# Loading k transposed by DMA in a long-convolution and token-MLP kernel

## The chip, the cores and the metric

One core of a Trainium2 chip runs the program. The metric is the time of one execution on the device, in microseconds (us); the kernel before takes 172.17 us (median of three runs, 172.11 to 172.44). The core has five engines that run side by side, each through its own list of instructions in order: TensorE (PE, matrix products; loading the stationary operand is shown as PEld), VectorE (DVE), ScalarE (ACT), GpSimd (POOL) and SyncE (SP, which here only issues DMA transfers). Products land in PSUM, which has eight banks; only DVE and ACT empty it into SBUF, the working memory of 128 partitions.

## The reference

What is computed, with S = 2048 tokens, D = 448 channels, F = 1792, all inputs bf16:

```python
x  = A_q                                   # [1, S, D]
# A: a four-tap filter along the tokens of k, a product with v, a long convolution, a gate
k_shift = sum(k_pad[:, t:t + S, :] * shift_k[:, 3 - t] for t in range(4))
kv = k_shift * v
y  = irfft(rfft(kv, 2 * S) * rfft(ssm_k, 2 * S))[:S] + kv * ssm_D     # per channel, along the tokens
h  = x + layernorm(x) * y
# B: an MLP over the tokens
n  = layernorm(layernorm(h))
u  = gelu(einsum("bsd,sf->bdf", n, w1) + b1)
h2 = h + transpose(einsum("bdf,fs->bds", u, w2) + b2)
```

## The kernel before

Token s = 16 q + r sits on partition q (0 to 127), in row r (0 to 15); so a tensor of 2048 x 448 is [128, 16, 448] in SBUF, and a load of four rows (a chunk, g = 0 to 3) moves 448 KB. The convolution is done as a two-step Fourier transform by table products on TensorE, with transfers inside SBUF between the steps (the shuffles, L1075 and L1202).

The steps carry tags, which the written order uses:

- `tables`: GpSimd and DVE make phase numbers (L838, L842, L845), ACT makes sines of them (L848, two halves of the table E, and L863).
- `kT`: the state kernel ssm_k (KN, [channel, token], four blocks of 128, 128, 128 and 64 channels) is turned by TensorE (L1038), eight rows to a PSUM bank, and emptied by `evac` (ACT L739, DVE L742) into KT.
- `kv`: the filter. L966 turns k (KH) into KX, channel on the partition: 48 transposes of 128 channels and 32 of 64; eight evictions (`kv.1` to `kv.8`) follow. L951 makes the 64 x 64 diagonals DG of the filter's taps, and L992 multiplies shifted stretches of KX by them, so that the filtered k comes out with the token on the partition; DVE multiplies it with v straight from PSUM (L1007), two instructions for each of eight chunks (four g, two halves cc of the channels). A zero column at the left of rows 13 to 15 stands for the tokens before the first.
- `k1`, `u1` (L1059): the first product of the transform, of the state kernel and of kv. Sixteen steps each, four products of 32 columns side by side; L1069 (ACT or DVE) empties two banks, and for the first four of `k1` L1067 (DVE) adds ssm_D. Every second step sends its shuffle (L1075), two transfers from GpSimd's queue and one from SyncE's.
- `k2`, `u2` (L1094): the second product, emptied by L739, L740, L742 and L743.
- `q`, `xn`: statistics of x (L1238, L1240) and its normalized rows (L1271 on ACT).
- `i1` (L1161, L1178), the shuffle back (L1202, L1189) and `i2` (L1304, L1310): the product of both transforms and the way back, with the gate and the second layernorm behind it.
- `mlp`: L1436 and L1446 (first matrix, GELU at L1426), L1458 (second matrix) and L1461, the final sum.

Which instruction comes when is written out by hand: the dictionary ORDER names, for each engine, every operation by step and number, and SLOTS gives each step its PSUM banks (two numbers a step, the second a bank or the first of a pair) and its ring buffers. The program computes only the waits. An engine never overtakes: an operation that waits holds up all that stand behind it in its list. `dummy` products (L1025) keep TensorE at work while nothing else is there.

SyncE's list begins with two chunks of k (0 and 1), the four blocks of the state kernel, ssm_D and the biases, the other chunks of k, v2, the filter, v3, v1 and v0. TensorE's list begins with nine dummies, the turning of the first k chunks, then the state kernel:

```python
"dummy.0:1-9 kv.4:0-11 kv.3:0-7 kv.6:0-11 kv.5:0-7 kT.1:0-7 kT.0:0-3 kT.1:9-11 kT.0:4-7 kT.3:0-7 "
...
"k1.9:0-7 k1.12:0-7 k1.10:0-7 kv.1:0-7 kv.2:0-11 k1.11:0-7 k1.15:0-7 k1.14:0-7 k1.13:0-7 kT.4:0-7 "
"kv.8:0-11 kv.12:0-23 kv.9:0-27 kv.10:0-23 kv.11:0-27 k1.4:0-7 k1.0:0-1 u1.0:0-7 k1.0:2-7 u1.1:0-7 "
```

Of the kernel before, what the change touches and what calls it, by code (L numbers as in the profile page):

```python
# [36 lines left out]
    ),  # L37
    "act": (
# [9 lines left out]
    ),  # L48
    "dve": (
# [15 lines left out]
    ),  # L65
    "pool": (
# [512 lines left out]
def _build(nc, A_q, A_k, A_v, A_shift_k, A_ssm_k, A_ssm_D, B_w1, B_b1, B_w2, B_b2, out):  # L579
# [8 lines left out]
    R = 16  # L588
# [39 lines left out]
    o_BD = o_IH + 256  # L628
    o_SM = o_BD + 4 * 256
    SMALL = o_SM  # L630
    NSMALL = 4032

    ctx = ExitStack()
    with ctx:
# [886 lines left out]
```

## Time and profile before

| | |
|---|---|
| median of three runs | 172.17 us |
| the profiled execution | 171.71 us |
| its span, first to last instruction | 169.7 us |
| PE busy | 159.8 us (94%) |
| DVE busy | 104.1 us (61%) |
| ACT busy | 88.4 us (52%) |
| POOL busy | 60.4 us (36%) |
| granted TensorE clock | 1.00 |
| read from HBM | 22.05 MB |

The profile is of one execution. A group of instructions shows the source line, engine, operation, output and inputs with shapes, how often, the busy time, the mean of one in ns, and the idle time of the engine just ahead of it with what ended it. SBUF is one tensor here, named arena, and PSUM one, named ps. Busy shares are means over stages with different limits; what counts for an edit is the stage in which it lies. Rows on one engine may overlap, since the next instruction starts while the last one still drains.

### The profile page before, as it was taken

The page shows a single profiled execution, that of the slowest core. Times are in us where ns is not written, and L with a number is a line of the kernel's source. Part 1 is how long each engine was busy: PE and PEld are TensorE (multiplying, and loading weights), DVE is VectorE, ACT ScalarE, POOL GpSimd, SP SyncE. Part 2 cuts the span into 40 slices and gives each one's busy share as a digit, 9 for nine tenths or more (in the row PEclk, how much of TensorE's full clock was granted, in tenths as well). Part 3 has the DMA queues.
Part 4 walks back from the last instruction along what each step waited for, and adds up shares of the span by engine and source line. Part 5 has one row for each costly group of instructions (what it writes and reads, how often), then busy time and mean ns, then how long its engine had stood idle before and what let it go on. Part 6 is the DMA issues. An engine that isn't in the chain of part 4 may idle for free.

```text
span 169.7 us, 3575 instructions
## 1 busy us (share of the span) xinstructions
PE 159.8 (94%) x1419; PEld 93.5 (55%) x1419; DVE 104.1 (61%) x193; ACT 88.4 (52%) x128; POOL 60.4 (36%) x155
## 2 busy tenths in 40 slices
PE   6999999788998899979999999999999999999994
PEld 2786745324333343434455555555567777777783
DVE  7998998999999999999987730000003223132231
ACT  3597859789999999998976144102360000000000
POOL 8346717473780554695788540000000000000000
PEclk9999999999999999999999999999999999999999
DMA  5999899775648875666999999940000111101111
GB/s 161 421 351 366 264 287 346 272 271 211 208 121 280 288 210 152 191 187 210 393 394 400 420 423 422 415 180 0 0 0 4 54 54 54 54 0 58 54 54 54
DMA packets 15564, 35.15 MB, mean 207 GB/s; under 512 B 3804, under 2 KB 9644, under 8 KB 15548
## 3 DMA queue, kind: packets, MB, share of 16 engines
q1 hardware_dynamic: 12396, 28.26, 45.6%
q0 software_dynamic: 3008, 6.58, 12.2%
q8 instruction: 11, 0.18, 0.4%
q10 hardware_dynamic: 144, 0.08, 0.2%
q14 instruction: 5, 0.04, 0.1%
HBM read 22.05 MB, written 1.84 MB: 141 GB/s over the span
## 4 chain that ended last, share of the span: by engine, by line
PE 68%; ACT 13%; DMA 8%; POOL 4%; DVE 3%; issue 2%; DVEq 0%; ACTq 0%; POOLq 0%
PE ps L1458 25%; PE ps L1436 13%; PE ps L1446 12%; ACT arena L739 8%; DMA arena<-arena 8%; PE ps L1025 3%; POOL arena L1075 3%; ACT arena L1069 3%; PE ps L966 3%; PE ps L1310 3%; PE ps L1059 3%; PE ps L1038 3%; ACT arena L740 2%; PE ps L992 2%; PE ps L1178 2%
## 5 line engine op out<-in xcount | busy, mean ns | idle before, releaser
L1461 DVE SCALAR_TENSOR_TENSOR arena<-ps,arena 128x448 bf16<-128x448 f32 (+2 forms) x17 | 11.1, 656 | 55.9 <-PE ps L1458 55.9
L1458 PE MATMUL ps<-arena 128*128 128x448 bf16 (+2 forms) x238 | 42.7, 342 | 0.0
L1458 PEld LDWEIGHTS ps<-arena 128*128 128x128 bf16 x238 | 33.3, 145 | 9.5
L1436 PE MATMUL ps<-arena 128*128 128x448 bf16 x112 | 23.7, 353 | 0.1
L739 ACT CAST arena<-ps 128x896 bf16<-128x896 f32 (+1 forms) x29 | 23.3, 896 | 0.6 <-PE ps L1178 0.4
L1069 ACT CAST arena<-ps 128x896 bf16<-128x896 f32 x24 | 20.4, 913 | 5.4 <-PE ps L1059 5.1
L1446 PE MATMUL ps<-arena 128*128 128x448 bf16 x112 | 22.5, 352 | 0.0
L1075 POOL DMA_DIRECT2D arena<-arena x32 | 17.6, 555 | 13.7 <-ACT arena L1069 13.5
L1426 ACT ACTIVATE arena<-ps,arena 128x448 bf16<-128x448 f32 x14 | 7.9, 641 | 18.2 <-PE ps L1436 10.6
L1059 PE MATMUL ps<-arena 128*32 128x448 bf16 x256 | 14.8, 355 | 2.3 <-ACT arena L1069 0.9
L1161 DVE TENSOR_TENSOR arena<-arena 128x1792 bf16<-128x1792 bf16 x16 | 16.6, 1082 | 0.2
L1436 PEld LDWEIGHTS ps<-arena 128*128 128x128 bf16 x112 | 10.8, 98 | 10.6 <-DVE arena L1389 0.7
L1446 PEld LDWEIGHTS ps<-arena 128*128 128x128 bf16 x112 | 11.0, 98 | 10.2
L1094 PE MATMUL ps<-arena 128*64 128x448 bf16 x128 | 15.1, 359 | 0.9 <-ACT arena L739 0.4
L1178 PE MATMUL ps<-arena 64*128 64x448 bf16 x128 | 14.1, 351 | 1.4 <-ACT arena L739 0.7
L1202 POOL DMA_DIRECT2D arena<-arena x16 | 9.3, 588 | 12.7 <-ACT arena L739 12.7
L1094 PEld LDWEIGHTS ps<-arena 128*64 128x64 f16 x128 | 5.6, 108 | 9.8 <-ACT arena L739 2.8
L1358 ACT ACTIVATE arena<-arena 128x448 bf16<-128x448 f32 x14 | 8.0, 572 | 5.6 <-DVE arena L1330 5.4
L1059 PEld LDWEIGHTS ps<-arena 128*32 128x32 f16 x256 | 5.3, 95 | 9.7 <-ACT arena L1069 2.5
L1178 PEld LDWEIGHTS ps<-arena 64*128 64x128 f16 x128 | 5.3, 94 | 9.7 <-DVE arena L1161 3.6
L1238 DVE BATCH_NORM_STATS2 arena<-arena 128x6 f32<-128x448 bf16 x16 | 9.6, 610 | 0.0
L1389 DVE TENSOR_SCALAR arena<-arena 128x448 bf16<-128x448 f32 x16 | 7.8, 507 | 2.7 <-POOL arena L1382 2.7
(98 smaller groups left out, 192.5 us busy)
## 6 DMA issues: line engine op xcount, KB each, us to landing
arena<-in_B_w_dram SPq DMA_DIRECT2D x8, 896.0 KB, 10.0
arena<-in_B_w_dram SPq DMA_DIRECT2D x2, 2048.0 KB, 17.3
arena<-arena SPq DMA_DIRECT2D x16, 224.0 KB, 3.5
arena<-arena POOLq DMA_DIRECT2D x32, 112.0 KB, 3.5
arena<-in_B_w_dram SPq DMA_DIRECT2D x2, 1536.0 KB, 19.2
arena<-arena POOLq DMA_DIRECT2D x13, 196.0 KB, 4.6
arena<-in_A_k_dram SPq DMA_DIRECT2D x4, 448.0 KB, 5.3
arena<-in_A_v_dram SPq DMA_DIRECT2D x4, 448.0 KB, 8.5
```

The costliest lines, as they stand in the source:

```text
L739: return e.copy(out=dst(), in_=src())
L1059: op("pe", lambda e, W, b=b, r=r, q=q, x=x, c0=c0: e.matmul(PS[32 * q:32 * q + 32, b.slots[x], 0:D], E[:, 2 * r + x, c0:c0 + 32], src[:, r ...
L1069: return e.copy(out=dst, in_=Ppair(b)) if W == "act" else e.tensor_copy(out=dst, in_=Ppair(b))
L1075: shuf[tag].append(op(q_, lambda e, W, g=g, i=i, a=a, nu=nu, jh=jh: e.dma_start(T[a + i:a + i + 4 * nu - 3:4].rearrange("p (j k) c d -> p ...
L1094: op("pe", lambda e, W, b=bs[h], h=h, j=j, c=c, par=par: e.matmul(PS[64 * par:64 * par + 64, b.slots[c], 0:D], FW[:, 64 * c:64 * c + 64], ...
L1161: op("dve", lambda e, W, m=m, i=i: e.tensor_tensor(out=MR(m.slots[0]).rearrange("p (x y) d -> p x y d", x=2), in0=TU[:, i].unsqueeze(2).br ...
L1178: k = op("pe", lambda e, W, b=bs[h], m=ms[h], par=par, t=t, tab=tab, xy=xy, P=P: e.matmul(Pb(b, par), tab[P, :], MR(m.slots[0])[P, xy, :], ...
L1238: op("dve", lambda e, W, bs=bs, r=r: e.bn_stats(out=bs, in_=XR(r)), r=[(oX(r), DB)], w=[(ob, 24)], n=D, kind="1x")
L1436: op("pe", lambda e, W, r=r, fc=fc, b=bs[fc]: e.matmul(Pb(b), W1A[:, r, 128 * fc:128 * fc + 128], Q[:, r, :], start=(r == 0), stop=(r == R ...
L1446: op("pe", lambda e, W, r=r, fc=fc, b=b: e.matmul(Pb(b), W1B[:, r, 128 * (fc - n0):128 * (fc - n0) + 128], Q[:, r, :], start=(r == 0), sto ...
L1458: op("pe", lambda e, W, r=r, fc=fc, b=b, d0=d0, d1=d1: e.matmul(Pb(b)[:, d0:d1], W2[fc // 7][:, fc % 7, r:S:R], G[:, fc, d0:d1], start=(fc ...
L1461: op("dve", lambda e, W, r=r, b=b, A=A, d0=d0, d1=d1: e.scalar_tensor_tensor(out=XR(r)[:, d0:d1], in0=Pb(b)[:, d0:d1], scalar=bm[:, r:r + ...
```

## The change

k is no longer loaded with the token on the partition. Four DMA transfers on SyncE's queue, behind the state kernel and the filter, write it transposed into KX, at the place of KH: a chunk of four rows is [128 tokens, 4 x 448 columns], cut into 14 groups of 128 columns; each group's 128 columns land on the partitions and its 128 tokens side by side. So the 80 transposes on TensorE and their eight evictions go away. As 448 is 7 x 64, a block of 64 channels lies on the lower or the upper half of the partitions by the parity of 7 (r mod 4) + block. The filter products are therefore made for seven blocks of 64 channels (49 a chunk of rows, 196 in all, 208 before), those with an even row offset first and those with an odd one behind them, since the halves change places between the two; an odd one's start waits for the even ones of its buffer (`after=evens[cc]`). The filter taps come as [64, 7, 4] on both halves by two transfers; the 28 diagonals are made by DVE (four blocks) and GpSimd (three). The four loads of v are issued by GpSimd instead of SyncE. The dummies' operand is smaller.

```diff
             for h in range(2):
-                op(Dq, lambda e, W, h=h: e.dma_start(wsn[64 * h:64 * h + 64, 3], A_shift_k[384:448]),
-                   w=[(o_wsn + 24, 8, "ws")], dmab=512)
+                op(Dq, lambda e, W, h=h: e.dma_start(wsn[64 * h:64 * h + 64], A_shift_k.rearrange("(b p) j -> p b j", p=64)),
+                   w=[(o_wsn, 56, "ws")], dmab=3584)
+            op("pool", lambda e, W: e.memset(KX[:, 3, 3:14, 15:16], 0.0),
...
-                    op(Dq, lambda e, W, c=c: e.dma_start(KH[:, 4 * c:4 * c + 4, :], k2d[:, 4 * c:4 * c + 4, :]),
-                       w=[(o_KH + 4 * c * DB, 4 * DB)], dmab=128 * 4 * DB)
+                    op(Dq, lambda e, W, c=c: e.dma_start(
+                        KX[:, c, :, 16:KW], k2d[:, 4 * c:4 * c + 4, :].rearrange("q r d -> q (r d)"), transpose=True),
+                       w=[(o_KH + 2 * KW * (14 * c + g) + 32, 256) for g in range(14)], dmab=128 * 4 * DB)
                 else:
-                    op(Dq, lambda e, W, c=c: e.dma_start(V[:, 4 * c:4 * c + 4, :], v2d[:, 4 * c:4 * c + 4, :]),
+                    op("pool", lambda e, W, c=c: e.dma_start(V[:, 4 * c:4 * c + 4, :], v2d[:, 4 * c:4 * c + 4, :]),
...
+        def kx(r, b):
+            f = 7 * (r % 4) + b
+            return f % 2, f // 2, o_KH + 2 * KW * (14 * (r // 4) + f // 2)
...
             for g in range(4):
+                bs = [_Buf(psum, 2) for _ in range(2)]
+                evens = [(), ()]
+                for od in range(2):
+                    for cc in range(2):
+                        b = bs[cc]
+                        for dl in ((-3, -1, 1, 3) if od else (0, -2, 2)):
+                            for bl in range(4 * cc, 4 * cc + 4 if cc == 0 else 7):
...
+                                hf, gr, ok = kx(rs, bl)
+                                P = slice(64 * hf, 64 * hf + 64)
+                                k = op("pe", lambda e, W, ...: e.matmul(
+                                    PS[:, b.slots[bl % 2], o:o + 64 * (i1 - i0 + 1)], KX[P, q, gr, sh:sh + 128],
+                                    DG[P, bl, i0 - dl:i1 - dl + 1, :].rearrange("p j d -> p (j d)"), ...),
+                                   ..., mode=3, after=evens[cc] if od else ())
...
+                op("pe", lambda e, W: e.matmul(Pb(dumb), DUM, DUM[:, 0:1].broadcast_to([128, D]), start=True, stop=True),
```

ORDER and SLOTS are new for all engines. The begin of each list after the change, with runs of numbers joined (`kv.1`, `kv.2` are the even products of chunk 0, `kv.3`, `kv.4` its odd ones with the multiplications by v, `kv.5` to `kv.8` those of chunk 1, and so on; `loads.5`, `.6`, `.8` and `.10` are k chunks 3, 0, 1 and 2; `loads.7`, `.9`, `.11` and `.12` the chunks of v):

```python
"sp":   "loads.0:0 loads.1:0 loads.2:0 loads.3:0 loads.4:0-1 loads.5:0 loads.6:0 loads.8:0 loads.10:0 loads.13:1 loads.14:0-1 k1.9:11 ..."
"pe":   "dummy.0:1-9 kT.1:0-7 kT.2:0-3 kT.3:0-7 kT.5:0-7 kT.2:4-7 kT.4:0-7 kT.6:0-7 kT.7:0-7 kT.1:9-11 kT.0:0-3 k1.8:0-7 k1.9:0-7 "
        "kT.3:9-11 kT.0:4-7 k1.10:0-7 k1.11:0-7 k1.12:0-7 kT.5:9-11 k1.13:0-7 k1.14:0-7 kv.1:0-11 kv.2:0-8 kv.3:0-15 kv.4:0-7 "
        "kv.6:0-7 kv.4:8-11 kv.6:8 k1.15:0-7 kv.8:0-7 kv.9:0-7 kv.8:8-11 kv.9:8-11 kv.11:0-15 kv.5:0-11 u1.0:0-7 kv.7:0-15 u1.1:0-7 ..."
"act":  "tables.0:5 tables.6:3 kT.5:8 tables.7:5 kT.6:8 kT.4:8 k1.9:8 kT.0:8 k1.11:8 k1.12:8 k1.14:8 tables.5:3 k1.15:8 u1.0:8 ..."
"dve":  "dummy.0:0 tables.3:0 kv.0:1 tables.3:1 tables.4:16-20 tables.6:0-2 tables.7:6 kT.1:8 tables.5:0 kT.3:8 tables.7:4 kT.2:8 "
        "kT.7:8 tables.7:7 kv.0:2 k1.8:8 tables.5:1 k1.10:8 tables.5:2 k1.13:8 kv.3:17 kv.3:16 kv.4:12-13 kv.8:13 kv.8:12 ..."
"pool": "... tables.2:11 loads.7:0 loads.9:0 q.0:1 q.0:0 tables.7:0 loads.11:0 tables.2:4 tables.2:8 tables.7:1 tables.2:6 "
        "tables.7:3 kv.0:0 loads.12:0 kv.0:3 k1.9:9 tables.7:9 k1.9:10 ..."
```

More of the change, by code (lines that the diff above doesn't have):

```diff
@@ L917, in emit_xload @@
                    w=[(oX(4 * c), 4 * DB)], dmab=128 * 4 * DB, after=shuf["u"] if c > 1 else ())
-        o_wsn = small(32)
-        o_wsc = small(64)
-        wsn = view(o_wsn, [4, 4])
-        wsc = view(o_wsc, [16], f32)
+        o_wsn = o_TT + 16384
+        o_wsc = o_wsn + 64
+        wsn = view(o_wsn, [7, 4])
+        wsc = view(o_wsc, [28], f32)
         o_b1n = small(256)
@@ L943, in emit_kv @@
             sch.t0 = -39.0
-            op("pool", lambda e, W: e.tensor_copy(out=wsc, in_=wsn.rearrange("p c j -> p (c j)")),
-               r=[(o_wsn, 32)], w=[(o_wsc, 64)], n=16)
-            for i in range(2):
-                op("pool", lambda e, W, i=i: e.memset(KX[i][:, :, 13:16, 7:8], 0.0),
-                   w=[(o_KX[i] + 272 * (16 * c + r), 16) for c in range(2) for r in range(13, 16)], est=34.0)
+            op("pool", lambda e, W: e.tensor_copy(out=wsc, in_=wsn.rearrange("p b j -> p (b j)")),
+               r=[(o_wsn, 56)], w=[(o_wsc, 112)], n=28)
@@ L975, in emit_kv @@
-            for g in range(4):
-                for cc in range(2):
-                    sch.t0 = T_KV + T_DKV * (2 * g + cc)
-                    b = _Buf(psum, 2)
-                    for i in range(2):
-                        one = 2 * cc + i == 3
-                        for m in range(5 if one else 7):
-                            for t in range(2):
-                                dl = ((0, -3, -2, -1, 1), (2, -1, 0, 1, 3))[t][m] if one else (0, -3, -2, -1, 1, 2, 3)[m]
-                                lo, hi = (2 * t, 2 * t + 1) if one else (0, 3)
-                                i0 = max(lo, dl)
-                                i1 = min(hi, dl + 3)
+            for q_, b0, nb in (("dve", 0, 4), ("pool", 4, 3)):
+                op(q_, lambda e, W, b0=b0, nb=nb: e.tensor_tensor(
+                    out=DG[:, b0:b0 + nb].rearrange("p b j d -> p (b j) d"), in0=I2.unsqueeze(1).broadcast_to([128, 4 * nb, 64]),
+                    in1=wsc[:, 4 * b0:4 * b0 + 4 * nb].unsqueeze(2).broadcast_to([128, 4 * nb, 64]), op=ALU.mult),
+                   r=[(o_I2, 128), (o_wsc, 112)], w=[(o_DG + 512 * b0, 512 * nb)], n=256 * nb, est=1700.0)
@@ new lines, in emit_kv @@
+            for g in range(4):
+                bs = [_Buf(psum, 2) for _ in range(2)]
+                evens = [(), ()]
+                for od in range(2):
+                    for cc in range(2):
+                        sch.t0 = T_KV + T_DKV * (2 * g + cc) + 1.5 * od
+                        b = bs[cc]
+                        for dl in ((-3, -1, 1, 3) if od else (0, -2, 2)):
+                            for bl in range(4 * cc, 4 * cc + 4 if cc == 0 else 7):
+                                i0 = max(0, dl)
+                                i1 = min(3, dl + 3)
@@ L987, in emit_kv @@
                                 rs = 4 * g + dl
[L988 removed]
+                                sh = 16 if rs >= 0 else 15
                                 rs %= R
[L990 to L997 removed]
@@ new lines, in emit_kv @@
+                                P = slice(64 * hf, 64 * hf + 64)
+                                o = 128 * (bl & 2) + 64 * i0
+                                k = op("pe", lambda e, W, b=b, bl=bl, cc=cc, q=rs // 4, dl=dl, i0=i0, i1=i1, sh=sh, o=o, P=P, gr=gr: e.matmul(
+                                    PS[:, b.slots[bl % 2], o:o + 64 * (i1 - i0 + 1)], KX[P, q, gr, sh:sh + 128],
+                                    DG[P, bl, i0 - dl:i1 - dl + 1, :].rearrange("p j d -> p (j d)"),
+                                    start=(dl == 0 and bl < 4 * cc + 2), stop=(dl == 3 and bl in (2, 3, 5, 6))),
+                                   r=[(ok + 30, 258), (o_DG + 512 * bl, 512)], bw=[b], n=64 * (i1 - i0 + 1),
+                                   est=8.0 + 13.5 * (i1 - i0 + 1), mode=3, after=evens[cc] if od else ())
@@ new lines, in emit_kv, with fn @@
+                                if not od:
+                                    evens[cc] = (k,)
+                        if not od:
+                            continue
+                        for c in (2 * cc, 2 * cc + 1):
+                            def fn(e, W, b=b, g=g, c=c):
+                                if c < 3:
+                                    v = V[:, 4 * g:4 * g + 4, 128 * c:128 * c + 128].rearrange("p r (t d) -> p t r d", t=2)
+                                    u = PS[:, b.slots[0]:b.slots[1] + 1, 256 * (c & 1):256 * (c & 1) + 256]
+                                    return e.tensor_tensor(out=v, in0=u.rearrange("p t (r d) -> p t r d", d=64), in1=v, op=ALU.mult)
+                                v = V[:, 4 * g:4 * g + 4, 384:448]
+                                u = PS[:, b.slots[0], 256:512]
+                                return e.tensor_tensor(out=v, in0=u.rearrange("p (r d) -> p r d", d=64), in1=v, op=ALU.mult)
+                            nb = 256 if c < 3 else 128
+                            rv = [(o_V + (4 * g + r) * DB + 256 * c, nb) for r in range(4)]
+                            op("dve", fn, r=rv, w=rv, br=[b], n=2 * nb, kind="psum")
```

67 lines of the change are left out of this document (10 added, 57 removed), and 250 rows, old and new, of tables (ORDER, SLOTS).

## The prediction

> **What bounds the kernel now.** I read the page's chain, then busy time by stretch, then the chain in order of time (start, length, what). A stretch shows its length, the busy us and number of instructions of PE, PEld, DVE, ACT and POOL, the granted clock, the busy share of the DMA engines and GB/s.
>
> ```profile
> PE 68%; ACT 13%; DMA 8%; POOL 4%; DVE 3%; issue 2%; DVEq 0%; ACTq 0%; POOLq 0%
> ```
>
> ```profile
> 0.00:25.00 25.00, 23.50 (x375) 16.03 (x379) 22.78 (x43) 16.63 (x19) 13.78 (x60) 1.00 0.91 306
> 25.00:50.00 25.00, 22.28 (x348) 9.96 (x336) 24.25 (x37) 21.99 (x27) 16.53 (x34) 1.00 0.70 249
> 50.00:78.00 28.00, 24.84 (x222) 10.67 (x223) 27.78 (x48) 26.66 (x35) 13.70 (x25) 1.00 0.66 201
> 78.00:170.00 92.00, 89.14 (x484) 56.86 (x482) 29.29 (x68) 23.12 (x51) 16.42 (x39) 1.00 0.44 170
> ```
>
> ```profile
> 4.92 2.76 PE ps L966 x40
> ...
> 13.21 0.45 PE ps L966 x8
> 13.65 1.63 PE ps L1059 x32
> 15.28 1.12 PE ps L966 x20
> ...
> 18.68 0.57 PE ps L966 x12
> 19.24 3.23 PE ps L992 x104
> ...
> 46.11 3.77 DMA arena<-arena
> ...
> 50.19 1.09 DVE arena L1161
> ...
> 72.79 3.72 DMA arena<-arena
> ...
> 76.56 1.70 PE ps L1310 x8
> ```
>
> PE's 68% misleads. From 78 on PE is full (89.14 of 92 us) with the MLP, which the edit leaves alone: its end moves as its start at 76.56 moves. Ahead of that the limits change. To 22.5 the chain is PE in order, 4.9 us of it the turning of k (L966, four rows). From 25 to 78 DVE is busy 52.0 of 53 us and ACT 48.7, emptying PSUM; two shuffles (46.11, 72.79) separate the stages. So the change is worth what it moves the work of DVE and ACT up to 72.8. The granted clock is 1.00 throughout.
>
> **The change, part by part.**
>
> ```profile
> L742 DVE COPY arena<-ps 128x1024 bf16<-128x1024 bf16 x11 | 7.1, 684 | 0.4 <-PE ps L1038 0.3
> L739 ACT COPY arena<-ps 128x1024 bf16<-128x1024 bf16 x3 | 2.8, 1021 | 3.5 <-PE ps L966 3.5
> L743 DVE TENSOR_SCALAR arena<-ps 128x896 bf16<-128x896 f32 x7 | 7.3, 1084 | 0.1
> L1069 ACT CAST arena<-ps 128x896 bf16<-128x896 f32 x24 | 20.4, 913 | 5.4 <-PE ps L1059 5.1
> L1238 DVE BATCH_NORM_STATS2 arena<-arena 128x6 f32<-128x448 bf16 x16 | 9.6, 610 | 0.0
> L1240 DVE BATCH_NORM_AGGREGATE arena<-arena 128x2 f32<-128x6 f32 x16 | 2.4, 166 | 0.0
> ```
>
> *Removed:* 80 turns on PE (4.9 us) and their eight evictions: three on ACT (2.8 us), five on DVE (5 x 0.684 = 3.4 us). The 6.2 us of the two busy engines are the prize; shared evenly, 3.1 us. But the written order changes everywhere, so I follow it engine by engine.
>
> *To the first filter multiplication on DVE (L1007).*
>
> ```profile
> 2.23 1.22 DVE L838 TENSOR_TENSOR arena<-arena 128x1024 int32<-128x1024 int32 x1
> ...
> 6.00 1.22 DVE L845 TENSOR_SCALAR arena<-arena 128x2048 int32<-128x2048 int32 x1
> ...
> 14.96 1.09 DVE L1069 CAST arena<-ps 128x896 bf16<-128x896 f32 x1 [0.57 <-PE ps L1059]
> ...
> 18.71 1.29 DVE L742 COPY arena<-ps 128x1024 bf16<-128x1024 bf16 x2 [0.34 <-PE ps L1038]
> 20.06 4.34 DVE L1007 TENSOR_TENSOR arena<-ps,arena 128x512 bf16<-128x512 f32 x8
> 24.32 2.22 DVE L1067 TENSOR_TENSOR arena<-ps,arena 128x896 bf16<-128x896 f32 x2
> ```
>
> ```profile
> L848 ACT ACTIVATE arena<-arena 128x2048 f16<-128x2048 int32 x2 | 3.9, 2020 | 0.0
> L863 ACT ACTIVATE arena<-arena 128x384 f32<-128x384 int32 x1 | 0.6, 617 | 0.0
> L1271 ACT ACTIVATE arena<-arena 128x448 f32<-128x448 bf16 x4 | 2.9, 763 | 0.0
> ```
>
> DVE first multiplies at 20.06. Its list ahead of that loses five k copies (-3.4) and four state-kernel copies that go to ACT (three full, one half: -2.4), and gains two evictions of the first product (+2.2). The 0.9 us of waiting in the rows goes; the small operations now put ahead of L838 delay the sine tables by about 1.1 us (estimate). That is 20.06 - 3.4 - 2.4 + 2.2 - 0.9 + 1.1 = 16.7. ACT's list is longer: sine tables at 7.2 (when L845 ends) 2.02, a copy 1.02, the small sine 0.62 and a wait of 0.3, copies 0.51 and 1.02, an eviction 0.91, a copy 1.02, an eviction 0.91: 15.5. Then PE does eight products (a quarter of 1.63, 0.41), so the filter products start at about 16.1; 37 of them at 3.23/104 = 0.031 and a switch of 0.37 give 17.6. Work in one queue overlaps (five L742 and L1007 rows last less than their mean times count), so I take 17.3 between 16.7 and 17.6: 2.8 us earlier.
>
> *From there to the shuffle at 72.79.* Before, four chunks (1.085 each, 4.34 by 4) lead to the first L1067 at 24.32; after, five: 17.3 + 5.4 = 22.7, a lead of 1.6. DVE's list from there to the last L1161 differs by one chunk less (-1.1), one eviction more (+1.1), two L743 less (-2.2), three statistics more (3 x 0.78 = +2.3) and small ones (+0.2): +0.3. DVE's lead is 1.3.
>
> ```profile
> 23.02 4.20 ACT L1069 CAST arena<-ps 128x896 bf16<-128x896 f32 x5 [2.41 <-PE ps L1059]
> ...
> 27.81 0.70 PEld L992 LDWEIGHTS ps<-arena 64*128 64x128 bf16 x24 [0.37 <-issue]
> ```
>
> On ACT the second of these five (23.86) empties the first product of kv. After, two more first-product evictions, the second half of the sine tables and one more eviction bring ACT from 15.5 to 15.5 + 1.8 + 2.02 + 0.91 = 20.3, and two chunks end at 19.5, early enough. A lead of 3.5, of which the list to the last i1 eviction takes two evictions more (1.8) and one L1271 pulled ahead (0.8): 0.9 stays. The smaller lead decides: **-0.9 us**.
>
> *Even and odd.* 196 products take the place of 208 (-0.4 us of PE), but odd ones of a chunk wait for its even ones: eight switches at up to 0.37, +3.0 at worst. PE idles 5.9 us between 25 and 78 and DVE takes 1.085 a chunk, so I cost it at nothing more; if PE became short there it would be these 3.0.
>
> *The loads.* SyncE issues the state kernel first, then filters, then k, one instruction per chunk of 448 KB; GpSimd issues v, four at about the 0.555 of its L1075, where it idled. No row shows a transposing transfer. The nearest are two stretches of the start, the time to landing of the four loads of k (L899), the queue with the smallest packets, and the issues.
>
> ```profile
> 0.00:4.00 4.00, 2.62 (x8) 1.07 (x9) 2.84 (x7) 1.49 (x2) 3.42 (x37) 1.00 0.54 150
> 4.00:7.00 3.00, 3.00 (x35) 2.01 (x33) 3.00 (x7) 1.04 (x2) 0.75 (x8) 1.00 1.03 416
> ```
>
> ```profile
> DMA to landing us min/median/max: 3.7/5.3/6.9
> ```
>
> ```profile
> q10 hardware_dynamic: 144, 0.08, 0.2%
> arena<-in_A_k_dram SPq DMA_DIRECT2D x4, 448.0 KB, 5.3
> L1075 POOL DMA_DIRECT2D arena<-arena x32 | 17.6, 555 | 13.7 <-ACT arena L1069 13.5
> ```
>
> By 7.0 the engines had moved 0.60 + 1.25 = 1.85 MB, as much as the state kernel (1.84), so k begins at about 7.4 (its last part uses half the partitions). Landing adds 0.8: k's first chunk (0.46 MB, past by about 3.6) landed 3.7 after its issue at 0.73. Fast end: 1.84 MB at 416 GB/s, 4.4 us. Slow end: pieces of 256 B at the smallest packets' time (0.2% of 16 x 169.7 us over 144 = 38 ns): 7168 pieces on 16 engines, 17.0 us. I take 4.4, as the nearest row is the plain load of the same bytes on the same queue. With all of v (4.4) alongside, the last chunk lands at 7.4 + 4.4 + 4.4 + 0.8 = 17.0. PE needs it when the third chunk's products start, 29 kv products, 16 others and a few waits behind 17.3: about 18.8. The cover is 1.8 us: up to 6.2 us for k (296 GB/s) nothing is late; beyond, each microsecond stalls PE, and behind PE the first products of kv, one for one.
>
> One rule speaks against the change. The Trainium skill, page "DMA: Bandwidth & Descriptors", section "Latency and other measured facts", gives a transposing transfer 261 GB/s where the source is strided; by it k takes 7.0 us, is 0.8 late, and 171.3 becomes 172.1. No row here shows the rate; the plain load's 416 does not contradict it.
>
> *Sum.* The profiled execution took 171.71 (169.7 span, 2.0 around it); 171.71 - 0.9 = 170.8. The median of the runs, 172.17, lies 0.46 above: **171.3**.
>
> **The rivals.**
> *A, k lands late (slower).* Place: PE's wait at the third chunk of the filter products. It decides once k takes over 6.2 us. At half the plain rate (8.8 us) it is 2.6 late: 171.3 + 2.6 = 173.9; at the slow end 10.8 late: 182.1. For it: DMA is 0.91 busy in the first 25 us, v now shares these engines, and pieces get small. Against: the same bytes took 5.3 us to land among other loads. The skill's 261 above lies just past the point.
> *B, the lead is lost again.* The list of ACT holds 2.6 us more from the first kv product on, and i1 starts only after the last shuffle (3.77 at 46.11), whose evictions are emptied in another order; if DVE and ACT wait on PSUM banks a microsecond more, 172.2. For it: ACT already idles on PE 5.4 us in L1069.
> *C, the prize in full.* All 6.2 us shared between both engines: 172.17 - 3.1 = 169.1. For it: DVE has no idle after 25. Against: ACT's longer list.
> *D, GpSimd holds things up.* Its cast of the filters stands ahead of v's last load, of its half of the diagonals and of all shuffles; if the filter load, in 896 pieces, is late as k was at most (6.9), a microsecond or two is lost: 172.9.
>
> **How the numbers follow.** A measurement of this kernel tells no change from a change at 0.2%, 0.34 us. Forecast 0.38 (its own range 170.3 to 172.1), A 0.26, B 0.18, C 0.10, D 0.08. Faster: 0.33 of the forecast, C, and 0.03 of B: 0.46. Same: 0.04 of the forecast and 0.10 of B: 0.14. Slower: A, D, 0.05 of B and 0.01 of the forecast: 0.40. The range goes from C, 169.2, to A with k at about 11 us, 176.5; about 0.14 lies outside.
>
> **What would show it.** Right: the weight load of the third filter chunk waits for no DMA; DVE's first multiplication near 17.3, the first of i1 near 49.3, the MLP's start near 75.7. Wrong: PE idle on a load of k between 16 and 25 (A); the first multiplication early but i1 at 50 or later (B); ACT waiting for DVE's tables or GpSimd's shuffles before 16 (D); or the MLP's start moving by less than the end.

## The result, and the profile after

| | before | after |
|---|---|---|
| median | 172.14 us | 174.40 us |
| lowest and highest | 171.48, 172.44 us | 174.16, 174.46 us |
| ratio to before, 95% interval | | 1.0132 [1.0094, 1.017] |
| profiled execution, its span | 171.71, 169.7 us | 174.34, 172.1 us |
| PE, DVE, ACT, POOL busy | 159.8, 104.1, 88.4, 60.4 us | 157.4, 100.7, 88.0, 65.1 us |

The changed kernel is slower by 2.3 us, where 0.9 us faster was forecast. One of its four executions took 187.86 us; the table and the ratios below leave out executions that far above a kernel's others, while the ranges given in the text include them. Lines are now those of the changed kernel: L982 is the transposing load of k, L986 the load of v, L1054 the filter products, L1069 and L1072 their multiplications by v, L1103 the turns of the state kernel, L1124 the first product with its evictions L1132 and L1134, L1226 the product of i1, L1501 the MLP's first matrix, L925, L928, L938 to L950 the tables, L1028 and L1033 the taps and the diagonals.

The chain's shares, from the page, and busy time by the same four stretches as before:

```profile
PE 58%; ACT 14%; DVE 10%; POOL 7%; DMA 7%; issue 2%; DVEq 0%; POOLq 0%; ACTq 0%
```

```profile
0.00:25.00 25.00, 20.60 (x292) 13.23 (x296) 20.49 (x35) 14.47 (x15) 19.05 (x62) 0.93 1.04 289
25.00:50.00 25.00, 22.02 (x331) 9.10 (x319) 23.78 (x41) 21.68 (x26) 18.08 (x37) 1.00 0.76 266
50.00:78.00 28.00, 24.09 (x225) 10.31 (x221) 26.08 (x42) 27.12 (x34) 13.23 (x22) 1.00 0.65 199
78.00:170.00 92.00, 90.71 (x491) 57.78 (x491) 30.28 (x71) 24.77 (x53) 14.77 (x39) 1.00 0.44 169
```

The work did go away: PE, DVE and ACT are all less busy in the first stretch (23.50 to 20.60, 22.78 to 20.49, 16.63 to 14.47). But they wait instead, and GpSimd, 13.78 before, is at 19.05. The chain in order of time (start, length, what) shows what for:

```profile
3.91 1.25 POOL arena L938
5.16 2.08 POOL arena L890 x3
7.24 0.74 POOL arena L986
7.99 0.57 POOL arena L986
...
8.70 0.62 POOL arena L938
9.32 0.54 POOL arena L986
...
10.76 1.01 POOL arena L942
11.79 0.36 DVE arena L944
12.15 0.93 DVE arena L825 x2
13.08 0.96 DVE arena L950
14.04 1.13 DVE arena L1033
15.18 1.00 DVE arena L1134
```

To 11.76 us the chain is GpSimd's list: table operations with three issues of v among them. Then DVE, whose L944 needs GpSimd's L942. The timeline with the waits, of DVE and ACT's L946, and SyncE's:

```profile
11.79 0.36 DVE L944 TENSOR_SCALAR arena<-arena 128x384 int32<-128x384 int32 x1 [2.18 <-POOL arena L942]
...
12.18 0.61 ACT L946 ACTIVATE arena<-arena 128x384 f32<-128x384 int32 x1 [2.27 <-DVE arena L944]
...
20.24 1.89 DVE L1069 TENSOR_TENSOR arena<-ps,arena 128x512 bf16<-128x512 f32 x3
...
25.77 3.14 DVE L1132 TENSOR_TENSOR arena<-ps,arena 128x896 bf16<-128x896 f32 x3
...
51.10 1.09 DVE L1226 TENSOR_TENSOR arena<-arena 128x1792 bf16<-128x1792 bf16 x1 [0.46 <-DMA arena<-arena]
```

```profile
4.13 12.20 SPq L982 DMA_TRANSPOSE arena<-in_A_k_dram  x4
```

Behind L944 in DVE's list stand evictions of the state kernel that PE had finished, and in ACT's list the same stand behind L946, which needs L944. The first filter multiplication comes at 20.24: 0.2 later than before, and 2.9 later than forecast. No filter product waits for k in this execution; but SyncE is held 12.2 us by four issues. The MLP's first product starts at 81.9 (first row below), 79.46 before, and from there both kernels take 90.2 us to the end of the span. The second row is the largest of those that count the waits ahead of the filter products by what ended them; none of these rows names a DMA.

```profile
L1501 PE MATMUL ps<-arena x112: 352/353/363, 81.9 to 121.5; 128*128 128x448 bf16 x112
```

```profile
  PE ps L1054: 1.0, 3
```

### The profile page after: what moved, and what is told of

The parts are those of the page before. It is cut to its first block, busy times and chain, and to the rows that moved or that the text cites. A ratio compares the mean times of both kernels' runs of the same rounds, so it can differ in the third digit from the quotient of the medians.

```text
span 172.1 us, 3375 instructions
## 1 busy us (share of the span) xinstructions
PE 157.4 (91%) x1327; PEld 90.4 (53%) x1327; DVE 100.7 (58%) x186; ACT 88.0 (51%) x127; POOL 65.1 (38%) x159
## 3 DMA queue, kind: packets, MB, share of 16 engines
HBM read 20.21 MB, written 1.84 MB: 128 GB/s over the span
## 4 chain that ended last, share of the span: by engine, by line
PE 58%; ACT 14%; DVE 10%; POOL 7%; DMA 7%; issue 2%; DVEq 0%; POOLq 0%; ACTq 0%
PE ps L1523 24%; PE ps L1501 12%; PE ps L1511 12%; ACT arena L822 10%; DMA arena<-arena 7%; PE ps L1054 3%; ACT arena L1134 3%; PE ps L1124 3%; DVE arena L1134 2%; PE ps L1375 2%; POOL arena L1140 2%; DVE arena L1069 1%; ACT arena L823 1%; POOL arena L890 1%; POOL arena L938 1%
## 5 line engine op out<-in xcount | busy, mean ns | idle before, releaser
L822 ACT CAST arena<-ps 128x896 bf16<-128x896 f32 x28 | 23.3, 963 | 0.4 <-PE ps L1159 0.4
L1501 PE MATMUL ps<-arena 128*128 128x448 bf16 x112 | 23.0, 353 | 0.1
L1140 POOL DMA_DIRECT2D arena<-arena x32 | 18.3, 576 | 11.7 <-ACT arena L1134 8.6
L1511 PE MATMUL ps<-arena 128*128 128x448 bf16 x112 | 21.8, 353 | 0.0
L1134 ACT CAST arena<-ps 128x896 bf16<-128x896 f32 x21 | 18.0, 915 | 5.3 <-PE ps L1124 3.9
L1124 PE MATMUL ps<-arena 128*32 128x448 bf16 x256 | 15.3, 356 | 2.3 <-DVE arena L825 0.8
L1226 DVE TENSOR_TENSOR arena<-arena 128x1792 bf16<-128x1792 bf16 x16 | 16.6, 1080 | 0.5 <-DMA arena<-arena 0.5
L1501 PEld LDWEIGHTS ps<-arena 128*128 128x128 bf16 x112 | 10.9, 98 | 10.7 <-DVE arena L1454 0.6
L1243 PE MATMUL ps<-arena 64*128 64x448 bf16 x128 | 13.8, 351 | 1.2 <-DVE arena L1226 0.9
L1267 POOL DMA_DIRECT2D arena<-arena x16 | 9.2, 582 | 14.4 <-ACT arena L822 14.1
L1124 PEld LDWEIGHTS ps<-arena 128*32 128x32 f16 x256 | 4.9, 95 | 9.8 <-ACT arena L1134 2.8
L823 ACT ACTIVATE arena<-ps 128x896 bf16<-128x896 f32 x11 | 9.5, 940 | 0.5 <-PE ps L1159 0.5
```

The lines of the kernel that those rows point to most:

```text
L822: return e.copy(out=dst(), in_=src())
L823: return e.activation(out=dst(), in_=src(), func=ACT.Copy, scale=scale)
L1124: op("pe", lambda e, W, b=b, r=r, q=q, x=x, c0=c0: e.matmul(PS[32 * q:32 * q + 32, b.slots[x], 0:D], E[:, 2 * r + x, c0:c0 + 32], src[:, r ...
L1134: return e.copy(out=dst, in_=Ppair(b)) if W == "act" else e.tensor_copy(out=dst, in_=Ppair(b))
L1140: shuf[tag].append(op(q_, lambda e, W, g=g, i=i, a=a, nu=nu, jh=jh: e.dma_start(T[a + i:a + i + 4 * nu - 3:4].rearrange("p (j k) c d -> p ...
L1226: op("dve", lambda e, W, m=m, i=i: e.tensor_tensor(out=MR(m.slots[0]).rearrange("p (x y) d -> p x y d", x=2), in0=TU[:, i].unsqueeze(2).br ...
```

## The experiments

The theory after the first look: GpSimd's late L942 blocks the heads of DVE's and ACT's lists. The rivals: the transposes themselves; the granted clock, which is 0.57 between 8 and 12 us, behind two idle times of PE (0.50 and 1.22 us); and the new written order behind 25 us. Ratios are to the kernel before, with 95% intervals.

### Four single changes to the changed kernel

**e1: L944 and L946 moved behind the evictions they held up.**

```diff
-"dve": "... kT.3:8 tables.7:4 kT.2:8 kT.7:8 tables.7:7 kv.0:2 ..."
+"dve": "... kT.3:8 kT.2:8 kT.7:8 tables.7:7 tables.7:4 kv.0:2 ..."
-"act": "... kT.5:8 tables.7:5 kT.6:8 kT.4:8 k1.9:8 ..."
+"act": "... kT.5:8 kT.6:8 kT.4:8 tables.7:5 k1.9:8 ..."
```

> The changed kernel with two instructions moved back in their lists: DVE's L944, which waited 2.18 us for GpSimd's L942, goes from ahead of three evictions to behind them, and ACT's L946, which waited 2.27 us for L944, behind two evictions. Nothing else changes. Theory (GpSimd's late L942 blocks the heads of both queues): the state kernel's copies go out as their products end, at about 10 to 11 instead of 12.06 to 14.2, and the first filter multiplication moves from 20.24 to about 18; as DVE is full from there on, the time falls from 174.4 by 1.5 to 2.3 us, to 172.1 to 172.9. Rival (clock): TensorE's products of the state kernel end at 11.2 at a granted clock of 0.57 and set the pace themselves; the gain is under 0.7. Rival (SyncE held by the transposes) and rival (the order behind 25 us): no gain, 174.2 to 174.6.

**e2: GpSimd issues v behind its table operations.**

```diff
-"pool": "... loads.7:0 loads.9:0 q.0:1 q.0:0 tables.7:0 loads.11:0 ... tables.7:3 kv.0:0 loads.12:0 kv.0:3 ..."
+"pool": "... q.0:1 q.0:0 tables.7:0 ... tables.7:3 loads.7:0 loads.9:0 loads.11:0 loads.12:0 kv.0:0 kv.0:3 ..."
```

> The changed kernel with GpSimd's four issues of v's loads (L986, 0.54 to 0.74 us each) moved behind its table operations, so that L942, at 10.76, is ready some 2 us earlier; v then lands some 2 us later, still ahead of 20. Theory (GpSimd): DVE's L944 runs at about 9.6 instead of 11.79, the first filter multiplication at about 18, the time 172.1 to 172.9, as in the run that moves L944 instead. If the issues are not what makes L942 late but the iotas beside DVE's table operations (L890, 2.08 us for three at 5.16), L942 comes at most 1.3 earlier and the gain is under 1. Rivals (clock, SyncE, later order): 174 or more.

**e3: k by plain copies.**

```diff
-KX[:, c, :, 16:KW], k2d[:, 4 * c:4 * c + 4, :].rearrange("q r d -> q (r d)"), transpose=True)
+KX[:, c, :, 16:KW], k2d[:, 4 * c:4 * c + 4, :].rearrange("q r d -> q (r d)").rearrange("q (g t) -> q g t", t=128))
```

> The changed kernel with k's four loads as plain copies of the same bytes to the same places, in pieces of 256 B: the transposition is left out, so the filter sees k unturned. Rival (SyncE held by the transposes, 12.2 us in its queue and the copies' small packets): ssm_D and the first shuffles leave SyncE 3 us earlier, the DMA engines are less full, and the time falls by 1 us or more, to 173.4 or less. Theory (GpSimd): the first filter multiplication stays at 20.2 and the time between 174.0 and 174.6.

**e4: nine more dummies in PE's gaps.**

```diff
-"pe": "... kT.1:0-7 kT.2:0-3 kT.3:0-7 kT.5:0-7 ..."
+"pe": "... kT.1:0-7 dummy.0:10-12 kT.2:0-3 kT.3:0-7 dummy.0:13-18 kT.5:0-7 ..."
```

> The changed kernel with nine more dummy products in TensorE's two gaps between 5.1 and 7.8 us (three behind the first eight turns of the state kernel, six behind the next twelve). Rival (clock): the granted clock stays at 1.00 in 8 to 12 us instead of 0.57, the 36 turns from 7.82 take 2.7 us instead of 3.44, and the time falls by 0.5 to 0.7 us, to 173.7 to 173.9. Theory (GpSimd): the turns end earlier, but their evictions stand behind DVE's L944 at 11.79 all the same; the first filter multiplication stays within 0.3 us of 20.24 and the time within 0.4 us of 174.4.

Measured: e1 174.82 to 187.89, ratio 1.0197 [1.0116, 1.0277]; e2 188.15 to 192.13; e3 174.28 (174.20 to 175.08), 1.0130 [1.0087, 1.0174]; e4 174.28 to 184.51. No version is faster than the changed kernel by more than these runs can tell. The timeline of PE and DVE in e2, and its L982 by source line:

```profile
31.89 1.06 PE L1054 MATMUL ps<-arena 64*128 64x256 bf16 x13 [12.26 <-DMA arena<-in_A_k_dram]
```

```profile
10.28 0.36 DVE L944 TENSOR_SCALAR arena<-arena 128x384 int32<-128x384 int32 x1 [0.79 <-POOL arena L942]
```

```profile
DMA to landing us min/median/max: 5.1/14.3/22.5
```

In e2 L942 is earlier, as the theory has it, and L944 waits 0.79 instead of 2.18. But k lands up to 22.5 us after its issue, v 15.7 to 17.8, and PE stands 12.26 us. In the profiled executions of e1 (187.89) and e4 (184.51) PE waits 10.3 and 6.9 us for k. So executions far above the median are put down to late transposes, this kernel's own (the one of 187.86 us was not profiled); e3, which has none, does not scatter. And e3 without transposes is as slow as the changed kernel: it looked as if the transposes were not what costs the 2 us where k is not that late. But e3 keeps the small pieces, to which e9 comes back, and its first multiplication, at 20.81, came 0.6 later than the changed kernel's: there the clock was down to 0.50 from 14 to 16 us.

### Plain copies, and v off GpSimd

**e5: e3 and e1 together.**

> Plain copies of k's bytes (the transposition left out, as in the run with plain loads) and L944 and L946 moved behind the copies they held up (as in the run that unblocks them). In the unblocked run with transposes TensorE waited 10.3 us for k; here no transposing transfer can be late. Theory (two causes: GpSimd's late L942 blocks both queues in every execution, and transposes beside v's transfers are late in some): the times lie close together and fall by 1.5 to 2.3 us from the 174.28 of plain loads alone, to 172.0 to 172.8; the first filter multiplication comes at about 18 to 19 instead of 20.8. Rival (the order behind 25 us costs the difference): the multiplication comes earlier but the time stays at 173.8 or more.

Measured: 174.68 (173.55 to 174.95), 1.0137 [1.0095, 1.0179]: no gain. The first multiplication came at 20.13, 0.7 ahead of e3's. The evictions went out earlier, but DVE's diagonals (L1033), beside GpSimd's own, took 2.99 us instead of 1.21, and the first L1134 began at 14.99 (15.10 in the changed kernel). The blocked heads alone are not the price; what GpSimd does beside DVE is part of it.

**e6 and e7: v on SyncE's queue (and out of GpSimd's list), ahead of k or behind it.**

```diff
-op("pool", lambda e, W, c=c: e.dma_start(V[:, 4 * c:4 * c + 4, :], v2d[:, 4 * c:4 * c + 4, :]),
+op(Dq, lambda e, W, c=c: e.dma_start(V[:, 4 * c:4 * c + 4, :], v2d[:, 4 * c:4 * c + 4, :]),
...
-"sp": "... loads.4:0-1 loads.5:0 loads.6:0 loads.8:0 loads.10:0 ..."
+"sp": "... loads.4:0-1 loads.7:0 loads.9:0 loads.11:0 loads.12:0 loads.5:0 loads.6:0 loads.8:0 loads.10:0 ..."   (e6)
+"sp": "... loads.4:0-1 loads.5:0 loads.6:0 loads.8:0 loads.10:0 loads.7:0 loads.9:0 loads.11:0 loads.12:0 ..."   (e7)
```

> The changed kernel with v's four loads on SyncE's queue ahead of k's transposes, not on GpSimd; the queue takes its transfers in order, so v is nearly through when the transposes start, and GpSimd is 2.4 us of issues lighter. Theory, first part (transposes are slow because v's packets run beside them): the landing times of the transposes lie close together, 4 to 8 us, no execution is above 177, though the last chunk may land 1 to 2 us after it is wanted. If the transposes are slow by themselves, k still lands 10 to 20 us after its issue and the times scatter up to 190. Theory, second part (GpSimd): without the issues L942 ends near 9 instead of 11.76 and L944 no longer waits 2.18 us; if k is in time, the time is 172.0 to 173.0.

> As the run before, but v's four loads behind k's transposes on SyncE's queue. k starts at about 7.4 with no v beside it, and v lands some 5 us later than in the changed kernel. Theory (v's packets beside the transposes make them slow): the transposes land 3 to 6 us after their issue, all by 16, and TensorE never waits for k; DVE's first multiplication waits for v instead, to 19 to 21, and the time is 172.5 to 174.5 without scatter. Rival (transposes slow by themselves): SyncE is held as before and k's last chunk lands at 20 or later, with scatter up to 190.

Measured: e6 179.05 (178.21 to 179.20), 1.0387 [1.0346, 1.0427]; e7 175.71 (175.01 to 176.39), 1.0209 [1.0169, 1.0249]. No scatter to 190 any more. In e7 PE never waits for k; DVE waits 0.67 us for v, the first multiplication comes at 19.94 and the first L1132 at 25.46, both 0.3 us ahead of the changed kernel, and yet the time is 1.3 us longer: from that L1132 to the MLP's first product e7 takes 57.9 us, the changed kernel 56.1. No run shows why. Stretches of e7 in which little but k's transposes runs (last columns: clock, DMA share, GB/s), and L982's time to landing:

```profile
8.00:10.00 2.00, 2.00 (x20) 1.91 (x19) 1.49 (x2) 1.93 (x2) 2.00 (x4) 0.50 1.14 206
10.00:12.00 2.00, 2.00 (x21) 1.40 (x20) 1.62 (x5) 1.33 (x3) 1.88 (x3) 0.50 1.08 218
12.00:14.00 2.00, 2.00 (x22) 0.96 (x20) 1.29 (x3) 0.67 (x1) 0.00 (x0) 0.50 1.10 210
```

```profile
DMA to landing us min/median/max: 5.0/6.2/6.7
```

In these stretches the engines are full (share over 1) and move 206 to 218 GB/s: half of the plain load's 416. k's 1.84 MB would take 8.7 us at that. In e6, behind v, they run into the time of the shuffles, and PE waits 1.38, 1.33 and 3.21 us for k. GpSimd's part shows here too: in both runs L944 waits 0.78 or 0.79 us, and in e6 DVE's last eviction ahead of the multiplications began at 17.27 instead of 19.07.

**e8: e6 with e1's moves.**

> v ahead of k on SyncE's queue, and in addition L944 and L946 behind the copies they held up. Theory (GpSimd's issues alone made L942 late): little over the run with v first alone, within 0.4 us of it. If the blocked heads still cost something there, up to 1 us less; if k's lateness decides, no difference.

Measured: 174.59 to 180.77; the profiled execution (180.77) has PE waiting 4.20 us for k. k decides; nothing can be read of the heads.

**e9: e6 with e3's plain copies.**

> Both suspects out at once: k's bytes by plain copies (the transposition left out), and v's loads on SyncE's queue ahead of them, so that GpSimd issues none. With v first and transposes, the last eviction of DVE ahead of the first filter multiplication began at 17.27, so the multiplication could start at 18.3 where k is there. Theory (the forecast's steps hold; late transposes and GpSimd are what it missed): multiplication at 18.3, 1 us behind the forecast's 17.3; first i1 multiplication at 50.3 or earlier; the time 171.3 + 1.0 = 172.3, at most 172.8. Rival (the written order behind 25 us costs the rest): the multiplication comes at 18.3 to 18.5 but the first of i1 still at 51 and the time at 173.8 to 174.4.

Measured: 175.49 (174.02 to 177.10), 1.0181 [1.0113, 1.0249]. A miss that taught the most: the multiplication came at 18.59, about as expected, and then PE waited 1.53 us for *plain* k. A plain copy in pieces of 256 B is late as well; e3 had not taken out the suspect.

**e10 and e11: all loads in one queue as they are wanted, transposing; e11 with e4's dummies.**

```diff
+"sp": "... loads.4:0-1 loads.5:0 loads.6:0 loads.7:0 loads.8:0 loads.9:0 loads.10:0 loads.11:0 loads.12:0 ..."
```

> The changed kernel, transposing, with all loads on SyncE's queue in the order in which they are wanted: state kernel, filter, k chunks 3 and 0, v chunk 0, k 1, v 1, k 2, v 2, v 3. In the run with v behind k, TensorE did not wait for k and the transposes moved some 210 GB/s between 8 and 14 us, so one chunk of 448 KB takes 2.2 us and one of v 1.1. Theory (transposes run at half the plain rate, and only then if nothing runs beside them): chunks 3 and 0 land at about 12.3, 1 at 15.5, 2 at 18.8, with v between; TensorE waits for k under 1 us, the first filter multiplication is at about 18.5, the time 172.5 to 174 without scatter. Rival (the transposes are slowed by v's packets in the same queue too): k's last chunk lands at 22 or later and the time is 176 or more.

> The run before with the nine more dummies in TensorE's gaps between 5.1 and 7.8 us. Theory (the clock falls to 0.57 between 8 and 12 us where TensorE has been idle, and costs 0.7 to 0.9 us of the state kernel's turns once GpSimd no longer delays their evictions): granted clock 1.00 up to 12 us, the turns end 0.8 us earlier, and the time is up to 0.8 us under the run before, where k is in time. If k or the later order decides, no difference.

Measured: e10 174.78 (174.59 to 177.27), 1.0164 [1.0129, 1.0200]; e11 175.37 (174.63 to 176.61), 1.0210 [1.0161, 1.0259]. In e11's timeline:

```profile
18.27 1.88 DVE L1069 TENSOR_TENSOR arena<-ps,arena 128x512 bf16<-128x512 f32 x3
```

```profile
22.00 2.71 PE L1054 MATMUL ps<-arena 64*128 64x256 bf16 x44 [2.17 <-DMA arena<-in_A_k_dram]
```

The front is 2 us earlier than in the changed kernel, and k takes them back at the third chunk of the filter products: rival A's place. These 44 products begin with `kv.9`, which reads k chunk 2, the last one loaded (issued at 14.22, with up to 7.6 us to landing).

In e10, without the added dummies, the front was not earlier. The clock was 0.50 from 8 to 14 us, and DVE waited for PE's first products of the transform:

```profile
14.51 1.09 DVE L1134 CAST arena<-ps 128x896 bf16<-128x896 f32 x1 [0.79 <-PE ps L1124]
...
16.54 1.09 DVE L1134 CAST arena<-ps 128x896 bf16<-128x896 f32 x1 [0.33 <-PE ps L1124]
...
20.26 1.89 DVE L1069 TENSOR_TENSOR arena<-ps,arena 128x512 bf16<-128x512 f32 x3 [0.50 <-PE ps L1054]
```

So the added dummies, which kept the clock at 1.00, went with a front 2 us earlier (in e10 the state kernel's turns also started 0.5 us later); the later k hid it in the time.

### k in pieces of 4 KB

The bytes of k are copied plain, one piece of 4032 B per partition and chunk (the transposition is left out; 12% more bytes), so that k cannot be late.

```diff
-KX[:, c, :, 16:KW], k2d[:, 4 * c:4 * c + 4, :].rearrange("q r d -> q (r d)"), transpose=True)
+KX[:, c].rearrange("p g t -> p (g t)"),
+    A_k[0].rearrange("(q r) d -> q (r d)", r=R)[:, max(0, 1792 * c - 224):max(0, 1792 * c - 224) + 2016])
...
```

**e12: e11 with these pieces. e13: the changed kernel with these pieces.**

> The run before (all loads on SyncE's queue in the order wanted, nine more dummies) with k's bytes in one plain piece of 4 KB per partition and chunk instead of transposed pieces of 256 B (the transposition is left out; 12% more bytes). In the run before, DVE was ready for the first filter multiplication at 18.27 and the third chunk of k came 2.17 us late. Theory (small pieces, not lack of room on the engines, make k late; GpSimd and the clock are out of the way already): no wait for k, five multiplied chunks by 23.7, the first of i1 at 50.0 or earlier, the time at most 172.8; if also the last stages cost nothing, 171.8. Rival (the order behind 25 us costs all of it): the first of i1 at 51 or later, or the MLP's first product more than 30 us behind it, and 173.8 or more.

> The changed kernel with only k's loads made plain, one piece of 4 KB per partition and chunk (the transposition left out); v stays on GpSimd. Theory (in an undisturbed execution GpSimd makes the front late, so that k in small pieces is just in time): SyncE is held 3 us instead of 12, its first shuffle leaves at about 16, but the first filter multiplication stays at 20.0 to 20.3 and the time at 173.6 to 174.4. If k's small pieces cost by their share of the DMA engines (late shuffles, late q), the time falls to 173.5 or less.

Measured: e12 171.85 (171.22 to 173.31), 1.0009 [0.9981, 1.0037]; e13 174.17 (173.62 to 175.32), 1.0158 [1.0099, 1.0216]. Against e11 the pieces alone are worth 3.5 us; against the changed kernel 0.2, which is nothing that these runs can tell (by the ratios e13 is even 0.4 behind). Each cause hides behind the other. With k in time, e13 still has its first multiplication at 20.24: GpSimd's front.

**e15: e13 with e2's order. e17: e12 without the dummies. e16: e11 with k's first three chunks ahead of v.**

> The changed kernel with k plain in 4 KB pieces (the transposition left out) and GpSimd's four issues of v behind its table operations instead of among them. With k in 4 KB pieces alone the time was 174.17, L944 waited 2.18 us for L942 and the first filter multiplication came at 20.24. Theory (GpSimd's issues among the table operations make the front late, where k cannot be late): L944 waits under 1 us, the multiplication comes at 18.3 to 19, unless v, issued later, is not there; time 171.9 to 172.8. If GpSimd's front is not worth the 2 us, 173.6 or more.

> The run with all loads in one queue and k plain in 4 KB pieces, without the nine more dummies. Rival (clock): 0.57 in 8 to 12 us again, the state kernel's turns 0.7 us later, first multiplication at 19 and the time 0.5 to 0.8 us above the 171.85 of the run with dummies. Theory (GpSimd's issues are the whole of the late front): within 0.3 us of 171.85.

> A kernel that transposes k by DMA and computes the reference, with what was learnt: all loads on SyncE's queue, in the order k 3, 0, 1, v 0, 1, k 2, v 2, 3, and the nine more dummies. In the run with v 0 ahead of k 1, the third chunk was 2.17 us late at 22.00; here it has one chunk of v less ahead of it. Theory (a small-piece chunk takes 2.2 us alone, one of v 1.1): chunk 1 lands by 17, v 0 by 18.5, v 1 by 20, k 2 by 23, each about when it is wanted; first multiplication at 18.3 to 19, time 172.0 to 173.5. If v still slows the pieces, v or k is late by 1 to 2 us again and the time is 174 to 175.5.

Measured: e15 172.78 (172.20 to 174.04), 1.0061 [1.0032, 1.0090]; e17 171.88 (171.42 to 172.88), 0.9998 [0.9969, 1.0027]; e16 177.38 (176.13 to 178.59), 1.0305 [1.0244, 1.0366]. From e13 to e15 GpSimd's order alone is worth 1.4 us (first multiplication at 19.45), and from e13 to e17 v off GpSimd 2.3. By the ratios it is 1.7 and 2.8; e13's interval alone is 1 us wide to either side. What e15 still lacks is GpSimd's list again: the four issues now stand ahead of its cast of the filter taps (L1028), for which DVE's diagonals wait:

```profile
12.88 1.23 DVE L1033 TENSOR_TENSOR arena<-arena 128x1024 bf16<-128x1024 bf16 x1 [1.05 <-POOL arena L1028]
```

Without the dummies the clock falls (0.60 and 0.55 between 8 and 12 us) and the time does not change: with k in time, the clock is ruled out. For the changed kernel itself the answer rests on one execution: e4, with the dummies, took 174.28 where k was not late, as long as without them. DVE in e17:

```profile
10.28 0.36 DVE L944 TENSOR_SCALAR arena<-arena 128x384 int32<-128x384 int32 x1 [0.78 <-POOL arena L942]
...
11.49 0.57 DVE L950 TENSOR_SCALAR arena<-arena 128x128 f32<-128x128 int32 x1
...
18.38 1.88 DVE L1069 TENSOR_TENSOR arena<-ps,arena 128x512 bf16<-128x512 f32 x3
...
23.91 3.15 DVE L1132 TENSOR_TENSOR arena<-ps,arena 128x896 bf16<-128x896 f32 x3
```

```profile
L1226 DVE TENSOR_TENSOR arena<-arena x16: 1056/1081/1094, 49.1 to 68.6; 128x1792 bf16<-128x1792 bf16 x16
```

```profile
L1501 PE MATMUL ps<-arena x112: 352/352/363, 80.5 to 120.0; 128*128 128x448 bf16 x112
```

DVE multiplies and adds from 18.38 on without a wait. e16 was meant as the best order for a kernel that does transpose by DMA, and it failed. Its edit could not do what was expected of it: the late chunk of e11 was k chunk 2, and ahead of that one the same five loads stand in both runs. It was issued at 14.28, as in e11, and landed later; the stretches show the transposes at 165 and then 130 GB/s with no load of v issued yet, and PE waits 4.30 us.

```profile
8.00:10.00 2.00, 2.00 (x25) 1.56 (x24) 1.49 (x2) 1.70 (x2) 2.00 (x4) 1.00 1.37 165
10.00:12.00 2.00, 2.00 (x28) 1.66 (x31) 1.73 (x5) 1.64 (x4) 1.89 (x3) 1.00 0.67 130
```

```profile
24.07 3.24 PE L1054 MATMUL ps<-arena 64*128 64x256 bf16 x44 [4.30 <-DMA arena<-in_A_k_dram]
```

No version that computes the reference, the transposition included, came under the kernel before; even with k for free (e12, e17) the rest only equals it.

## Why the prediction was wrong

*PE full from 78 on: right.* 90.71 us busy of 92; the end moved with the MLP's start.

*The removed work: right,* but freed time on DVE and ACT was turned into waiting.

*The first filter multiplication at 17.3: this step failed.* It came at 20.24. Its term "GpSimd issues v, four at about the 0.555 of its L1075, where it idled", costed at nothing, was a place that GpSimd had before the change; in the new order three of the issues, and iotas that took 2.08 us for three, stand ahead of L942, for which DVE's and ACT's lists wait with evictions behind. In the sum's own terms, ACT's "wait of 0.3" at the small sine was 2.27 us, and DVE's list, given no wait at all, had 2.18 at L944. The changed order on GpSimd had to be followed like DVE's and ACT's. The runs size it: 1.4 us by the order alone (e15), 2.3 with v off GpSimd (e17). In e17 the multiplication is at 18.38, still 1.1 behind the forecast: L944 waits 0.78, and L950 takes 0.57 beside GpSimd's diagonals (0.28 before the change).

*The loads: the size was off by a factor of two.* k was taken at 416 GB/s and 4.4 us, "as the nearest row is the plain load"; alone it goes at 206 to 218 at best (e7), 8.7 us. That is rival A's half rate (8.8), far past its point of 6.2. In the changed kernel the shortest landing, 6.8 us, behind the last issue at 13.8 puts the last chunk at 20.6 or later, against a deadline of 18.8; in the profiled execution it did no harm only because the front was 2.9 us late. Once the front is early, k costs 3.5 us (e11 against e12). The two ends given, 4.4 and 17.0, held it; taking the row nearest in bytes, not in the size of the pieces, was the mistake. Here the Trainium skill, page "DMA: Bandwidth & Descriptors", section "Latency and other measured facts", was the better guide: its 261 GB/s for a strided source is nearer to the 206 to 218 than 416 is, though still too fast.

*From there to the shuffles, +0.3 on DVE's list: right.* From the first L1132 to the last product of i1 took 44.8 us after (25.77 to 70.6) and 44.5 before (24.32 to 68.8, second row).

```profile
L1226 DVE TENSOR_TENSOR arena<-arena x16: 1061/1083/1092, 51.1 to 70.6; 128x1792 bf16<-128x1792 bf16 x16
```

```profile
L1161 DVE TENSOR_TENSOR arena<-arena x16: 1056/1084/1093, 50.2 to 68.8; 128x1792 bf16<-128x1792 bf16 x16
```

*Even and odd at nothing: right.* Three switches cost PE 1.0 us, and in e17 DVE has no wait there.

*The rivals.* D had the sign that came true, ACT waiting for DVE's table before 16, but at too small a price (172.9) and with the filter's load as the cause. A had the rate and the place, and is what bounds a kernel whose front is mended. C did not come: even with k for free the time only reached 171.85. B, the lead lost again, stays open: the last product of i1 to the MLP's first took 10.7 us before, 11.3 after, and between 10.4 (e15) and 12.1 (e7) in the experiments. In e17 it took 11.9, which turns a lead of 0.2 us at the last product of i1 (68.6 against 68.8) into a delay of 1.0; but e17's profiled execution lies 0.7 us above its median, that of the kernel before 0.5 below, and no run changed this stage.

That 174.40 lies inside the range given is luck: the range reached that far for late k, and D, the rival nearest to what happened, stopped at 172.9.

So of the 3.1 us between forecast and result, GpSimd's front holds 2.3 (e13 to e17), k's pieces 0.2 that can't be told from nothing, and 0.6 is left between e17 and the forecast. By the ratios, which take out the difference between sessions, these are 2.8, -0.4 and 0.8; the split is good to about half a microsecond at best. Some 0.3 us of the first part lies outside the profiled span, where the forecast kept its "2.0 around it": time less span is 2.2 to 2.3 us in every execution of the kernels in which GpSimd issues v, and 1.9 to 2.1 in all others, the kernel before among them; no run shows the cause. What is late in e17 lies in the rest of the front and the last stage; the 0.6 is not divided further.

## What to carry to other kernels

A transfer that moves to another engine's queue costs that engine's list, in its new order: follow it to the first operation that others wait for. Cost a transfer by the size of its pieces, not by its bytes. And when taking out one suspect gains nothing, take out two together before dropping either: here each of two late things hid the other.

## What was not expected of the hardware

Transposing transfers do not keep a rate: with no load of v issued yet 206 to 218 GB/s in e7 and 130 to 165 in e16; beside v's loads from GpSimd's queue, e2 shows 50 GB/s in 14 to 16 us and landings of 22.5 us. The three kernels derived from the changed one that kept both (e1, e2, e4) scatter between 174.3 and 192.1.

Four issues in small pieces hold SyncE 12.2 us transposing and 11.4 us plain (e3); in 4 KB pieces 2.1 us (e13). So it is the small pieces, not the transposition, that hold the queue, and everything behind it.

GpSimd and DVE slow each other in some pairs of operations: three iotas took 2.08 us beside DVE's L925 and L928 (one tensor operand each), where five larger ones took 0.79 before, beside L838 (two operands):

```profile
3.24 0.79 POOL L807 IOTA arena<- 128x128 int32 x5
```

DVE's L1033 took 2.99 in e5, beside GpSimd's diagonals, and 1.21 in the changed kernel, behind them. The Trainium skill, page "SBUF — State Buffer", section "SBUF: two separate sides", says that the two share one pair of ports under an exclusive lock; these rows agree.

In ten of the thirteen profiled executions without the nine added dummies PE was granted only 0.50 to 0.55 of its clock in at least one stretch of 2 us between 8 and 16 us, in the changed kernel behind gaps of 0.50 and 1.22 us; in e2, e6 and e8 it was not. With the dummies (e4, e11, e12, e16) it stayed at 1.00 up to 16 us. The state kernel's 36 turns took up to 3.49 us instead of 2.53 to 2.60. Where evictions were held up anyway or k was in time, that cost nothing (e12 against e17); in e10 DVE waited for it.
